# Moving the four fp16 sums of each second-layer pair from VectorE to GpSimd in an attention and mixture-of-experts kernel

## Chip, cores, metric

One NeuronCore of one Trainium2 chip. The metric is the device time of one execution in microseconds (us); lower is better. In the profile PE is TensorE's matmuls, PEld its weight loads, DVE is VectorE, ACT is ScalarE, POOL is GpSimd, SP is SyncE. The granted clock is the share of its full clock that the profile shows TensorE was given. In this kernel matmuls write tiles in PSUM (their names end in `ps`); the other tiles named below lie in SBUF.

## The reference, cut to what matters

Linear attention makes x (4608 tokens by 512), then eight experts of two layers follow, each weighted by a gate P that a balancing loop has normalised:

```python
for e in range(E):                      # E = 8, D = 512, F = 1024
    h = np.maximum(x @ w1[e], 0.0)
    ye = h @ w2[e]
    out += P[:, e:e + 1] * ye
```

The argument is about experts 2 to 7 (counted from 0), which the kernel runs from about 330 us on.

## The kernel before

From expert 1 on, both layers use the seven-product form of a 2x2 block product (Strassen's, in Winograd's arrangement): seven products instead of eight, paid for with sums of operands. Each expert is 6 *units*. A unit is 4 *groups* of the first layer (seven products each) and 3 *pairs* of the second layer (a pair is two blocks of 128 tokens, seven products each). The pairs of one unit run interleaved with the groups of the next unit.

A pair needs four sums of first-layer outputs, all SBUF to SBUF in fp16:

```python
class Pair:
    ...
    def sums(self, earlier=None):
        ...                                     # S1, S2, S4: two buffers each
        for out_, in0, in1, op in (
            (S1[:], self.a21, self.a22, ALU.add),
            (self.a21, self.a11, self.a21, ALU.subtract),     # in place in H
            (S2[:], S1[:], self.a11, ALU.subtract),
            (S4[:], self.a12, S2[:], ALU.subtract),
        ):
            i = (nc.gpsimd if self.last else ve).tensor_tensor(
                out=out_, in0=in0, in1=in1, op=op
            )
            ...
```

So before the change only the very last pair has its sums on GpSimd. The products P7 (reads the in-place `a21`), P6 (S2), P5 (S1) and P3 (S4) follow in a fixed order on TensorE.

VectorE has other SBUF-to-SBUF sums: three for the second-layer weights of each expert (called *V sums* here; 128x1024, made at the expert's first pair), one difference in w2, and 16 for the first-layer weights (*w1 sums*, written to tiles T or in place to w1e; 128x256; 12 of them in the last unit of the expert before):

```python
        if name == "P1":
            if self.first:                      # first pair of an expert
                tw2[0:2] = [t_pool.tile(... name=f"V{k_}")[:] for k_ in (2, 3)]
                ve.tensor_tensor(out=tw2[0], in0=b22, in1=b12, op=ALU.subtract)
                ve.tensor_tensor(out=tw2[1], in0=tw2[0], in1=b11, op=ALU.subtract)
            self.mult(self.U, self.a11, b11, True)
            se.copy(out=self.W, in_=self.U)
            if not self.last:
                self.sums()
        elif name == "P7":
            if self.first:
                tw2[2:3] = [t_pool.tile(... name="V4")[:]]
                ve.tensor_tensor(out=tw2[2], in0=b21, in1=tw2[0], op=ALU.subtract)
            self.mult(self.V, self.a21, tw2[1], self.last)
        ...
```

A group ends its products in one PSUM bank Z (shown as `p_ps`), which VectorE empties twice with a fused add and relu before TensorE may go on there:

```python
        product(Z, T3, x_part(1, 0, n), True)
        add_relu(h22, Z, u4)          # VectorE: H <- relu(p_ps + u), line 744
        ...
        product(Z, T4, x_part(1, 1, n), False)   # in the next group
        add_relu(h21, Z, u2)
```

VectorE also adds each product, gated, to the result (`acc <- rows_ps, P_tok, acc`, line 814). From expert 1 on the order on each engine is chosen by the scheduler when the program is built; only dependencies bind it.

## Time and profile before

| | before |
|---|---|
| median of 2 runs | 987.89 us (987.68 to 988.11) |
| PE busy, 330 to 970 us | 639.87 of 640 us |
| DVE busy, same stretch | 545.12 us (85%) |
| POOL busy, same stretch | 7.42 us |

The page of the kernel before: engines' busy time over the span, and the first line of the chain that ended last.

```profile
PE 968.0 (98%) x7846; PEld 677.9 (69%) x7846; DVE 810.4 (82%) x1838; ACT 566.4 (57%) x1260; POOL 60.4 (6%) x82
...
PE 93%; DMA 2%; DVE 2%; ACT 1%; POOL 1%; issue 0%; DVEq 0%; POOLq 0%; ACTq 0%; SPq 0%
```

Windows of the kernel before: stretch, its length, busy time of PE, PEld, DVE, ACT, POOL (and instructions), granted TensorE clock, DMA share, GB/s. The first lies in mid-expert, the second holds the start of an expert's second layer.

```profile
434.00:440.00 6.00, 6.00 (x48) 4.52 (x47) 3.96 (x9) 3.04 (x8) 0.00 (x0) 1.00 0.35 101
440.00:446.00 6.00, 6.00 (x47) 4.35 (x46) 6.00 (x14) 3.49 (x9) 0.23 (x1) 1.00 0.00 0
```

TensorE has no gap in either, even where VectorE is busy for 6.00 of 6 us.

The sums that stay on VectorE, kernel before: nanoseconds minimum/median/maximum.

```profile
L846 DVE TENSOR_TENSOR V<-w2e x7: 680/681/684, 219.0 to 879.9; 128x1024 f16<-128x1024 f16 x7
L847 DVE TENSOR_TENSOR V<-V,w2e x7: 683/685/687, 220.0 to 880.9; 128x1024 f16<-128x1024 f16 x7
L856 DVE TENSOR_TENSOR V<-w2e,V x7: 680/684/687, 223.1 to 884.4; 128x1024 f16<-128x1024 f16 x7
...
L722 DVE TENSOR_TENSOR T<-w1e,T x24: 284/288/299, 301.1 to 862.0; 128x256 f16<-128x256 f16 x24
```

Timeline of the kernel before around the V sums of expert 3, VectorE: start, length, engine, line, operation, out<-in.

```profile
439.36 0.55 DVE L744 CUSTOM_DVE_ANT_0 H<-p_ps,u 128x384 f16<-128x384 f32 x1
439.83 0.47 DVE L814 SCALAR_TENSOR_TENSOR acc_lo<-rows_ps,P_tok,acc_lo 128x256 f32<-128x256 f32 x1
440.22 0.68 DVE L846 TENSOR_TENSOR V<-w2e 128x1024 f16<-128x1024 f16 x1
440.82 0.42 DVE L829 TENSOR_TENSOR hs<-H 128x512 f16<-128x512 f16 x1
441.15 0.69 DVE L847 TENSOR_TENSOR V<-V,w2e 128x1024 f16<-128x1024 f16 x1
441.75 0.42 DVE L829 TENSOR_TENSOR H<-H 128x512 f16<-128x512 f16 x1
442.09 0.42 DVE L829 TENSOR_TENSOR hs<-hs,H 128x512 f16<-128x512 f16 x1
442.42 0.55 DVE L744 CUSTOM_DVE_ANT_0 H<-p_ps,u 128x384 f16<-128x384 f32 x1
```

The same place on TensorE:

```profile
443.03 0.48 PE L109 MATMUL p_ps<-xT,T 128*128 128x384 f16 x2
```

VectorE runs two V sums, three pair sums (L829) and then the relu (L744), which is over at 442.97; the matmul into `p_ps` that waits for it starts at 443.03, on time. There is no slack left, but nothing is late.

### The profile page before, as it was taken

The page shows a single profiled execution, that of the slowest core. Times are in us where ns is not written, and L with a number is a line of the kernel's source. Part 1 is how long each engine was busy: PE and PEld are TensorE (multiplying, and loading weights), DVE is VectorE, ACT ScalarE, POOL GpSimd, SP SyncE. Part 2 cuts the span into 40 slices and gives each one's busy share as a digit, 9 for nine tenths or more (in the row PEclk, how much of TensorE's full clock was granted, in tenths as well). Part 3 has the DMA queues.
Part 4 walks back from the last instruction along what each step waited for, and adds up shares of the span by engine and source line. Part 5 has one row for each costly group of instructions (what it writes and reads, how often), then busy time and mean ns, then how long its engine had stood idle before and what let it go on. Part 6 is the DMA issues. An engine that isn't in the chain of part 4 may idle for free.

```text
span 987.4 us, 20228 instructions
## 1 busy us (share of the span) xinstructions
PE 968.0 (98%) x7846; PEld 677.9 (69%) x7846; DVE 810.4 (82%) x1838; ACT 566.4 (57%) x1260; POOL 60.4 (6%) x82
## 2 busy tenths in 40 slices
PE   7999999989999999999999999999999999999997
PEld 6445544447777777777777777777777777777775
DVE  5886774779889888988789888988789888988887
ACT  5756665467776555555555555555555555555551
POOL 6302110010000000000000000000000000000001
PEclk8999999999999999999999999999999999999999
DMA  9969981642013410133113400233103400104535
GB/s 168 206 99 154 160 153 26 125 67 67 26 48 68 75 42 25 38 79 67 42 33 68 88 29 25 51 66 68 49 25 68 92 25 27 48 25 114 131 86 128
DMA packets 80336, 73.54 MB, mean 74 GB/s; under 512 B 33264, under 2 KB 72176, under 8 KB 80240
## 3 DMA queue, kind: packets, MB, share of 16 engines
q0 software_dynamic: 27232, 30.94, 19.9%
q1 hardware_dynamic: 52768, 41.06, 16.9%
q8 instruction: 61, 1.00, 0.4%
q14 instruction: 35, 0.29, 0.1%
q10 hardware_dynamic: 240, 0.26, 0.1%
HBM read 83.12 MB, written 12.98 MB: 97 GB/s over the span
## 4 chain that ended last, share of the span: by engine, by line
PE 93%; DMA 2%; DVE 2%; ACT 1%; POOL 1%; issue 0%; DVEq 0%; POOLq 0%; ACTq 0%; SPq 0%
PE rows_ps L109 34%; PE h_ps L109 28%; PE copied_ps L109 11%; PE p_ps L109 11%; PE y_ps L109 5%; PE small_ps L109 4%; DMA v_ld<-in_v_dram 2%; DMA q_pT<-q_p 1%; DVE xT L109 0%; DVE acc_hi L814 0%; POOL hs_last L829 0%; DVE P_tok L109 0%; DMA out_dram<-acc_lo 0%; DVE colp L109 0%; ACT u L109 0%
## 5 line engine op out<-in xcount | busy, mean ns | idle before, releaser
L814 DVE SCALAR_TENSOR_TENSOR acc_lo<-rows_ps,P_tok,acc_lo 128x512 f32<-128x512 f32 (+1 forms) x322 | 203.7, 642 | 74.5 <-PE rows_ps L109 74.4
L109 PEld LDWEIGHTS <-H 128*128 128x128 f16 x2080 | 203.0, 98 | 83.1 <-issue 1.2
L750 ACT CAST u<-h_ps 128x384 f16<-128x384 f32 x288 | 137.8, 478 | 131.2 <-PE h_ps L109 130.6
L109 PEld LDWEIGHTS <-w1e 128*128 128x128 f16 x1632 | 156.3, 98 | 67.9 <-issue 7.8
L744 DVE CUSTOM_DVE_ANT_0 H<-p_ps,u 128x384 f16<-128x384 f32 x329 | 181.7, 552 | 6.6 <-PE p_ps L109 6.4
L109 PEld LDWEIGHTS <-hs 128*128 128x128 f16 x1500 | 146.6, 98 | 56.2
L109 PE MATMUL h_ps<-S,w1e 128*128 128x384 f16 x672 | 164.1, 326 | 1.1 <-ACT u L109 0.9
L109 PE MATMUL p_ps<-xT,T 128*128 128x384 f16 x672 | 164.1, 326 | 0.1
L109 PE MATMUL h_ps<-xT,w1e 128*128 128x384 f16 (+1 forms) x616 | 150.3, 351 | 1.4 <-DVE xT L109 1.3
L109 PE MATMUL rows_ps<-V,H 128*128 128x256 f16 x1000 | 150.0, 273 | 0.7 <-DVE acc_hi L814 0.7
L109 PE MATMUL rows_ps<-w2e,hs 128*128 128x256 f16 x1000 | 150.0, 273 | 0.0
L782 ACT ACTIVATE H<-h_ps 128x384 f16<-128x384 f32 x144 | 70.7, 491 | 95.0 <-PE h_ps L109 95.0
L109 PEld LDWEIGHTS <-T 128*128 128x128 f16 x1008 | 98.1, 98 | 29.2 <-issue 2.8
L109 PE MATMUL rows_ps<-w2e,H 128*128 128x256 f16 (+1 forms) x568 | 91.2, 285 | 0.0
L763 ACT COPY copied_ps<-h_ps 128x384 f32<-128x384 f32 x144 | 67.5, 468 | 35.2 <-PE h_ps L109 35.2
L773 ACT ACTIVATE H<-copied_ps 128x384 f16<-128x384 f32 x144 | 70.9, 492 | 20.3 <-PE copied_ps L109 20.3
L109 PE MATMUL h_ps<-S,T 128*128 128x384 f16 x336 | 81.8, 325 | 0.3 <-ACT copied_ps L109 0.3
L109 PE MATMUL copied_ps<-xT,w1e 128*128 128x384 f16 x336 | 82.1, 326 | 0.0
L109 PE MATMUL copied_ps<-w2e,H 128*128 128x256 f16 x504 | 75.5, 272 | 0.0
L109 PE MATMUL rows_ps<-V,hs 128*128 128x256 f16 x500 | 75.0, 272 | 0.0
L814 DVE SCALAR_TENSOR_TENSOR acc_lo<-copied_ps,P_tok,acc_lo 128x256 f32<-128x256 f32 x126 | 60.3, 479 | 0.4
L814 DVE SCALAR_TENSOR_TENSOR acc_hi<-rows_ps,P_tok,acc_hi 128x512 f32<-128x512 f32 (+1 forms) x56 | 41.3, 738 | 20.1 <-PE rows_ps L109 19.3
(135 smaller groups left out, 957.5 us busy)
## 6 DMA issues: line engine op xcount, KB each, us to landing
S<-x_saved SPq DMA_DIRECT2D x108, 192.0 KB, 2.4
out_dram<-acc_lo SPq DMA_DIRECT2D x62, 128.0 KB, 2.4
w1e<-in_moe_w_dram POOLq DMA_DIRECT2D x7, 1024.0 KB, 9.3
w2e<-in_moe_w_dram POOLq DMA_DIRECT2D x7, 1024.0 KB, 10.0
k_ld<-in_k_dram POOLq DMA_DIRECT2D x16, 288.0 KB, 8.4
v_ld<-in_v_dram POOLq DMA_DIRECT2D x16, 288.0 KB, 9.4
q_ld<-in_q_dram POOLq DMA_DIRECT2D x16, 288.0 KB, 7.8
x_saved<-S SPq DMA_DIRECT2D x18, 192.0 KB, 1.9
```

The source lines that it names most:

```text
L109: i = getattr(self.engine, name)(*args, **kwargs)
L744: latest = ve._custom_dve(TENSOR_ADD_SAT, out=out, in0=ps[:, 0:TU], in1=t[:], s0=FP32_MAX, s1=0.0)
L750: se.copy(out=t[:], in_=ps[:, 0:TU])
L763: se.copy(out=Y[:, 0:TU], in_=X[:, 0:TU])
L773: se.activation(out=h11, in_=Y[:, 0:TU], func=AF.Relu)
L782: se.activation(out=h12, in_=X[:, 0:TU], func=AF.Relu)
L814: ve.scalar_tensor_tensor(out=a, in0=rows, scalar=P_tok[:, g, self.e : self.e + 1], in1=a, op0=ALU.mult, op1=ALU.add,)
```

## The change

The intent is to relieve VectorE, the second busiest engine, by giving the four sums to GpSimd, which is nearly idle, from the third expert on (e = 2).

```diff
@@ -826,7 +826,7 @@
                 (S2[:], S1[:], self.a11, ALU.subtract),
                 (S4[:], self.a12, S2[:], ALU.subtract),
             ):
-                i = (nc.gpsimd if self.last else ve).tensor_tensor(
+                i = (ve if self.e == 1 else nc.gpsimd).tensor_tensor(
                     out=out_, in0=in0, in1=in1, op=op
                 )
                 if self.last and earlier is not None:
```

It moves 107 pairs, 428 instructions. In the built program the order of TensorE, ScalarE and SyncE is unchanged. On VectorE the scheduler now puts the three V sums in a row, all three ahead of the relu, and in the last unit of an expert it shifts some w1 sums, the w2 difference and a relu against each other. So the change has two parts, another engine and another order.

## The prediction

> **What bounds the kernel now.** TensorE. The busy-time windows give PE 99.97 of every 100 us between 300 and 900 us (DVE 85 to 87, ACT 56, POOL under 2); the chain of waits is 93% PE. A unit of three pairs and four groups takes 17.92 us in the timeline, 5.97 us a pair, with no PE gap. So the moved work is not on the critical path: VectorE waits for TensorE (83 us for rows_ps after 300 us, in the waits), never the other way round. There is nothing to gain beyond a fraction of a microsecond in the tail.
>
> **What moves.** 107 pairs (experts 2 to 7, the last pair being on GpSimd already) times four 128x512 fp16 sums: 0.42 us each on DVE, 1.15 us each for the four on POOL at the end of the trace. DVE loses about 180 us of busy time, POOL gains about 493 us: 4.7 of each 5.97 us. TensorE, ScalarE and DMA orders are unchanged; the two weight loads per expert stay in POOL's queue with tens of us to spare.
>
> **Latency.** Mid-unit pairs may start their sums 5 us early, so 4.7 us is hidden. A unit's first pair waits for the last relu of its H (513.1 us in the timeline): on POOL S2 ends about 3.5 us later, at 516.7; the matmul that needs it loads weights at 517.1. It just fits: 0 to 0.2 us lost.
>
> **Tail.** The last three pairs come 3.5 us apart there, but POOL needs 4.7 us for each. The last pair's sums start near 979.5 instead of 977.0: +2.5 us.
>
> **Port.** The Trainium skill ("SBUF — State Buffer", Who interferes with whom) says a DVE instruction with two SBUF inputs contends with a GpSimd instruction that reads SBUF, and that the second "fully blocks". The trace of before has no such overlap, so no run here shows it; during the last pair's POOL sums DVE ran accumulations with one PSUM input at normal length, which agrees with the rest of the rule. What is left on DVE with two SBUF inputs: per expert three V sums (0.68 us, now back to back in DVE's order, right where the first pair's sums run), one w2 difference (0.68), 16 w1 sums (0.29), these in the last unit and the start of the next, where DVE was already 17.8 of 18 us busy. If they take turns with 1.15 us POOL sums, each waits up to 1.15 us. Estimate: the three V's end about 3 us late (445.5 instead of 442.3), the relu behind them holds p_ps, and TensorE stalls about 3 us; six experts, 18 us. The 12 sums of the last unit stall it another 2 to 5 us, for five experts: 10 to 25 us. The accumulations and relus between have slack of 0.05 to 1 us only.
>
> **Time.** 987.9 + 2.5 (tail) + about 30 (port, stage boundaries) = 1020 us. Without the lock, 989 to 992. Range 991 to 1045. Chances: faster by over 2% 0.01, same 0.33, slower 0.66.
>
> **What would show it.** Right: DVE groups of V, w2e, T (w1) sums with means well above 0.68 and 0.29 us, up to 1.8 and 1.4; the STT and relu groups unchanged; PE idle on the relu into H (p_ps) in the units around each expert change, PE still 99.9% busy in the middle units; POOL about 50% busy; tail 2 to 3 us longer. Wrong: V and T sums at their old durations.
>
> **What would make it wrong.** No blocking, or DVE gets the port in the middle of a POOL sum: then only the tail remains. POOL sums longer than 1.15 us beside a busy DVE: a unit's first pair then has no slack, and every unit stalls. A GpSimd that keeps the port over consecutive sums: then stalls double.

## The result, and the profile after

| | before | after |
|---|---|---|
| median of 2 runs | 987.89 us (987.68 to 988.11) | 1028.38 us (1027.81 to 1028.94) |
| ratio | | 1.041, 95% interval 1.0365 to 1.0455 |
| granted TensorE clock, profiled run | 0.996 | 0.985 |

A ratio is the mean time of one kernel's fast runs over the mean time of the other's fast runs of the same rounds, so it is not quite the ratio of the medians. The change makes the kernel 40 us slower; a repeat on another chip gave 1027.37 us beside 989.63 us, ratio 1.0386.

The page after, the same two lines:

```profile
PE 984.6 (96%) x7846; PEld 683.3 (67%) x7846; DVE 718.7 (70%) x1410; ACT 567.5 (55%) x1260; POOL 556.5 (54%) x510
...
PE 76%; DVE 9%; POOL 7%; issue 4%; DMA 3%; ACT 1%; POOLq 0%; DVEq 0%; ACTq 0%
```

The same 7846 matmuls now show 984.6 us busy instead of 968.0, and the chain runs through VectorE and GpSimd for a sixth of the span. That chain does not yet say whose fault it is: it names GpSimd both where its sums are late and where VectorE stood waiting behind them.

Windows after; the start of expert 3's second layer now lies at 447 us.

```profile
440.00:446.00 6.00, 6.00 (x48) 4.47 (x47) 3.85 (x7) 3.09 (x8) 3.08 (x3) 1.00 0.24 68
446.00:452.00 6.00, 4.67 (x36) 3.37 (x35) 5.71 (x6) 2.97 (x7) 4.30 (x4) 1.00 0.12 34
452.00:458.00 6.00, 5.12 (x27) 3.36 (x27) 3.70 (x8) 1.45 (x3) 5.64 (x5) 0.72 0.00 0
458.00:464.00 6.00, 6.00 (x48) 4.51 (x47) 3.64 (x7) 3.50 (x8) 5.09 (x6) 1.00 0.73 100
```

In mid-expert TensorE is as gapless as before, with GpSimd making all the sums. At the start of the second layer it first stands still and then, in the next window, runs 27 matmuls instead of 48 at a mean granted clock of 0.72.

The sums that stayed on VectorE, after (answers to the four lines of before):

```profile
L846 DVE TENSOR_TENSOR V<-w2e x7: 681/1473/1537, 220.3 to 912.5; 128x1024 f16<-128x1024 f16 x7
L847 DVE TENSOR_TENSOR V<-V,w2e x7: 682/1523/1525, 221.2 to 914.0; 128x1024 f16<-128x1024 f16 x7
L856 DVE TENSOR_TENSOR V<-w2e,V x7: 681/1632/1634, 224.3 to 915.5; 128x1024 f16<-128x1024 f16 x7
...
L722 DVE TENSOR_TENSOR T<-w1e,T x24: 279/842/1076, 302.3 to 894.2; 128x256 f16<-128x256 f16 x24
```

Timeline after, VectorE, GpSimd and TensorE one after the other; the brackets give the idle time before an instruction and what ended it.

```profile
446.92 0.55 DVE L744 CUSTOM_DVE_ANT_0 H<-p_ps,u 128x384 f16<-128x384 f32 x1
447.38 0.47 DVE L814 SCALAR_TENSOR_TENSOR acc_lo<-rows_ps,P_tok,acc_lo 128x256 f32<-128x256 f32 x1
447.78 1.47 DVE L846 TENSOR_TENSOR V<-w2e 128x1024 f16<-128x1024 f16 x1
449.28 1.52 DVE L847 TENSOR_TENSOR V<-V,w2e 128x1024 f16<-128x1024 f16 x1
450.73 1.63 DVE L856 TENSOR_TENSOR V<-w2e,V 128x1024 f16<-128x1024 f16 x1
452.28 0.54 DVE L744 CUSTOM_DVE_ANT_0 H<-p_ps,u 128x384 f16<-128x384 f32 x1
```

```profile
447.55 1.15 POOL L829 TENSOR_TENSOR hs<-H 128x512 f16<-128x512 f16 x1 [4.39 <-DVE H L744]
448.78 1.48 POOL L829 TENSOR_TENSOR H<-H 128x512 f16<-128x512 f16 x1
450.22 1.59 POOL L829 TENSOR_TENSOR hs<-hs,H 128x512 f16<-128x512 f16 x1
451.89 1.48 POOL L829 TENSOR_TENSOR hs<-H,hs 128x512 f16<-128x512 f16 x1
```

```profile
450.19 0.49 PE L109 MATMUL h_ps<-xT,w1e 128*128 128x384 f16 x2
452.88 0.48 PE L109 MATMUL p_ps<-xT,T 128*128 128x384 f16 x2 [2.21 <-DVE H L744]
453.20 0.77 PE L109 MATMUL rows_ps<-V,H 128*128 128x256 f16 x4
453.76 0.85 PE L109 MATMUL h_ps<-S,T 128*128 128x384 f16 x2
```

Read the first two together. The V sum that starts at 447.78 inside a GpSimd sum is not done until 449.25, 0.55 us after that sum's end at 448.70. The GpSimd sum begun at 448.78 lasts 1.48 us instead of 1.15 and ends 1.01 us after the V sum. They take turns through all three V sums. VectorE works in order, so the relu behind them comes at 452.28, and the matmul that needs the emptied bank waits 2.2 us. The matmuls after it are longer (2 of 384 columns in 0.85 us instead of 0.48).

**Where the 40 us lie.** Both programs issue the same matmuls in the same order, so the k-th matmul of one trace can be set beside the k-th of the other. Between the 2000th matmul and the last, the delay grows by 38.1 us, in steps at three kinds of place:

| place | steps | each | sum |
|---|---|---|---|
| V sums, start of each second layer, experts 2 to 7 | 6 | 2.3 us waiting, then 1.6 us of half-speed matmuls | 23.3 us |
| last unit of experts 2 to 6, where the w1 sums are made | 5 | 2.3 us waiting (0.4 + 1.2 + 0.4 + 0.3) | 11.5 us |
| tail, last three pairs | 1 | 2.7 us | 2.7 us |

The sum is 37.5 us; the rest is in steps below 0.3 us and at the start and end of the span. The half speed is in the clock record: six stretches of 3.413 us at 0.5 of full clock, one behind each V place (3.413 x 0.5 = 1.7 us lost; 1.6 us shows in the matmuls). The trace of before has none from 30 us on but for the last instants.

The tail after, TensorE: the bracket names GpSimd, and here it is a late result, not a turn.

```profile
1013.90 0.61 PE L109 MATMUL rows_ps<-V,H 128*128 128x256 f16 x4 [0.66 <-POOL H L829]
1015.01 0.61 PE L109 MATMUL rows_ps<-V,hs 128*128 128x256 f16 x4 [0.50 <-POOL hs L829]
...
1018.71 0.61 PE L109 MATMUL p_ps<-V,H 128*128 128x256 f16 x4 [0.78 <-POOL H L829]
```

### The profile page after: what moved, and what is told of

Read it like the earlier page. It is cut to its first block, busy times and chain, and to the rows that moved or that the text cites. A ratio compares the mean times of both kernels' runs of the same rounds, so it can differ in the third digit from the quotient of the medians.

```text
span 1027.2 us, 20469 instructions
## 1 busy us (share of the span) xinstructions
PE 984.6 (96%) x7846; PEld 683.3 (67%) x7846; DVE 718.7 (70%) x1410; ACT 567.5 (55%) x1260; POOL 556.5 (54%) x510
## 4 chain that ended last, share of the span: by engine, by line
PE 76%; DVE 9%; POOL 7%; issue 4%; DMA 3%; ACT 1%; POOLq 0%; DVEq 0%; ACTq 0%
PE rows_ps L109 27%; PE h_ps L109 23%; PE copied_ps L109 9%; PE p_ps L109 9%; POOL hs L829 5%; PE y_ps L109 5%; PE small_ps L109 4%; DVE acc_lo L814 2%; POOL H L829 2%; DVE T L722 2%; DMA v_ld<-in_v_dram 2%; DVE H L744 1%; DMA k_ld<-in_k_dram 1%; DVE V L856 1%; DVE w1e L722 1%
## 5 line engine op out<-in xcount | busy, mean ns | idle before, releaser
L814 DVE SCALAR_TENSOR_TENSOR acc_lo<-rows_ps,P_tok,acc_lo 128x512 f32<-128x512 f32 (+1 forms) x322 | 206.4, 642 | 130.3 <-PE rows_ps L109 129.9
L829 POOL TENSOR_TENSOR hs<-H 128x512 f16<-128x512 f16 x107 | 123.8, 1157 | 164.8 <-DVE H L744 160.6
L109 PEld LDWEIGHTS <-hs 128*128 128x128 f16 x1500 | 148.7, 99 | 61.3 <-issue 3.9
L109 PE MATMUL p_ps<-xT,T 128*128 128x384 f16 x672 | 164.5, 326 | 21.2 <-DVE H L744 21.2
L829 POOL TENSOR_TENSOR hs<-H,hs 128x512 f16<-128x512 f16 x107 | 127.8, 1194 | 11.9 <-PE rows_ps L109 5.2
L829 POOL TENSOR_TENSOR H<-H 128x512 f16<-128x512 f16 x108 | 126.6, 1173 | 8.2
L829 POOL TENSOR_TENSOR hs<-hs,H 128x512 f16<-128x512 f16 x107 | 126.4, 1181 | 0.0
L127 POOL DMA_DIRECT2D w1e<-in_moe_w_dram x11 | 8.5, 773 | 167.4 <-PE h_ps L109 128.9
L109 PE MATMUL h_ps<-S,T 128*128 128x384 f16 x336 | 84.0, 332 | 0.4 <-ACT copied_ps L109 0.3
```

Of the source, the lines that this page charges most:

```text
L109: i = getattr(self.engine, name)(*args, **kwargs)
L127: nc.gpsimd.dma_start(out=w[0][:, :, f0:f1], in_=view[:, :, f0:f1])
L814: ve.scalar_tensor_tensor(out=a, in0=rows, scalar=P_tok[:, g, self.e : self.e + 1], in1=a, op0=ALU.mult, op1=ALU.add,)
L829: i = (ve if self.e == 1 else nc.gpsimd).tensor_tensor(out=out_, in0=in0, in1=in1, op=op)
```

## The experiments

Three theories were to be told apart:

- **Port**: VectorE instructions with two SBUF inputs and GpSimd's sums take turns; VectorE is thrown back, its relu is late, TensorE waits and, after a long wait, gets half clock.
- **Latency**: GpSimd's sums are 2.8 times as long as VectorE's (1.15 us against 0.42), so TensorE waits for their results.
- **Order**: the scheduler now puts three V sums in a row ahead of the relu; that alone makes it late, whatever GpSimd does.

Each kernel differs from the changed kernel or the kernel before in one point; quiet and quiet2 put several together. The diffs are set against the changed kernel or the kernel before, whichever is nearer. "Matmul lag" is the growth of the delay against the trace of before, measured as above, in us.

| run | median, beside before in the same rounds | ratio (95%) | V places | w1 places | tail | lag |
|---|---|---|---|---|---|---|
| changed kernel | 1028.38, 987.89 | 1.041 | 6 x 2.3, 6 half clocks | 5 x 2.3 | 2.7 | 38.1 |
| first_dve | 1007.09, 990.33 | 1.0173 (1.0158 to 1.0188) | 6 x 0.47 | 5 x 2.3 | 2.7 | 17.0 |
| first_only | 1007.84, 990.33 | 1.0184 (1.0165 to 1.0202) | 6 x 2.3, 2 half clocks | 0 | 0 | 17.2 |
| v4_late | 1008.23, 990.33 | 1.0181 (1.0166 to 1.0197) | 6 x 0.75 | 5 x 2.3 | 2.7 | 18.7 |
| no_v (wrong result) | 1004.55, 990.33 | 1.0142 (1.0127 to 1.0158) | 0 | 5 x 2.3 | 2.7 | 13.8 |
| write_only (wrong result) | 999.74, 989.68 | 1.0098 (1.0083 to 1.0113) | no stall of the relu | none of the relu | see text | 9.9 |
| read_one (wrong result) | 1053.27, 989.68 | 1.0635 (1.0617 to 1.0653) | see text | see text | 4.9 | 62.7 |
| unit_dve | 1009.72, 989.68 | 1.0198 (1.0183 to 1.0213) | 6 x 2.3, 2 half clocks | 0 | 2.7 | 20.2 |
| quiet | 992.74, 989.68 | 1.0027 (1.0012 to 1.0042) | 6 x 0.47 | 0 | 0 | 3.1 |
| quiet2 | 991.70, 989.63 | 1.0017 (1.0005 to 1.003) | 0 | 0 | 0 | 0.3 |
| tail_only | 993.12, 989.63 | 1.0036 (1.0023 to 1.005) | 0 | 0 | 2.8 | 2.8 |
| after_again (changed kernel) | 1027.37, 989.63 | 1.0386 (1.0372 to 1.04) | 6 x 2.3, 5 half clocks | 5 x 2.3 | 2.7 | 36.0 |

### first_dve: the first pairs back on VectorE

```diff
-                i = (ve if self.e == 1 else nc.gpsimd).tensor_tensor(
+                i = (ve if self.e == 1 or self.first else nc.gpsimd).tensor_tensor(
```

> As the changed kernel, but the sums of the first pair of each of experts 2 to 7 (6 pairs of 107) stay on VectorE, where they stood before. Theory (port): the three V sums no longer meet a GpSimd sum, so they are back at 0.68 us and the stall of 2.3 us and the 1.56 us of half clock behind it are gone at all six experts: 6 x 3.9 = 23 us less, about 1005 us; the 2.3 us at each of five w1 places and 2.7 us in the tail stay. Rival (latency: what TensorE waits for is GpSimd's slower sums themselves, everywhere a pair starts): 6 of 107 pairs changed, so at most a few us less, about 1025 us.

1007.09 us. Six pairs of 107 bring back 21 us of the 38 (lag 38.1 to 17.0). Latency is out as the main cause. The 2 us missing to 1005 have a reason of the same kind: the third V sum now meets the *second* pair's sums (1.23 us instead of 0.68) and 0.47 us is lost at each expert.

### first_only: only the first pairs on GpSimd

```diff
-                i = (nc.gpsimd if self.last else ve).tensor_tensor(
+                i = (nc.gpsimd if self.last or self.first and self.e > 1 else ve).tensor_tensor(
```

> As the kernel before, but the sums of those 6 first pairs (and of the last, as before) are on GpSimd, 101 pairs stay on VectorE. Port theory: V sums at about 1.5 us, six stalls of 3.9 us: 988 + 23 = 1011 us, no loss at the w1 places, no loss in the tail. Latency rival: 6 of 107 of the loss, about 990 us. If 1011 and first_dve at 1005 both hold, the cost sits wholly at these 6 pairs and adds.

1007.84 us; 17 us instead of the 23 expected. The six waits of 2.3 us are all there, with V sums of 1.47, 1.52 and 1.63 us as in the changed kernel, but half clock followed only two of them. So the waits belong to these six pairs, and the half clock is a matter of chance or phase; see after_again.

### v4_late: the order changed, GpSimd untouched

```diff
                 if self.first:
                     tw2[2:3] = [t_pool.tile([P, FH, DH], F16, name="V4")[:]]
-                    ve.tensor_tensor(out=tw2[2], in0=b21, in1=tw2[0], op=ALU.subtract)
+                    i = ve.tensor_tensor(out=tw2[2], in0=b21, in1=tw2[0], op=ALU.subtract)
+                    if self.e > 1:
+                        not_before(latest, i)
```

> As the changed kernel, all sums on GpSimd, but from the third expert on the third V sum is held behind the relu that stood behind it (order only, one edge). Port theory: two V sums still take turns with GpSimd, the relu comes 1.6 us earlier, so TensorE waits about 0.7 us instead of 2.3 us at each expert and the gap is too short to bring the half clock: 6 x 3.1 = 18 us less, about 1010 us; half-clock stretches gone from the trace. Latency rival: GpSimd's sums are untouched, so no change, 1028 us. If the half clock comes for another reason than the long gap, it stays and the time is about 1019 us.

1008.23 us: one ordering edge for one of three V sums is worth about 20 us (lag 38.1 to 18.7) with every pair sum still on GpSimd. The wait is 0.74 us at five experts and 0.81 at one, and no half clock follows. V sums two at a time are still 1.47 and 1.52 us. This refutes latency a second time, and shows that the harm is done through the relu behind the V sums.

### no_v: the V sums left out

```diff
-                if self.first:
+                if self.first and self.e == 1:      # at both places of V sums
```

> Wrong result on purpose: as the changed kernel, but the V sums of experts 2 to 7 are not made (those of expert 1 are used again), all pair sums on GpSimd. Port theory: nothing of VectorE with two SBUF inputs meets the first pair's sums; TensorE does not wait there: about 1005 us, with the w1 places (11.5 us) and the tail (2.7 us) left. Latency rival: the first pair's sums come as late as ever, so 1028 us less at most 1 or 2 us. This one does not tell the port from plain VectorE load; the runs with a GpSimd that only writes do.

1004.55 us, result wrong (relative error 1.95). No step is left at the V places; the w1 places and the tail are as they were. All first pairs still had their sums on GpSimd, so these do come in time.

### write_only: GpSimd writes but does not read

```diff
-                i = (ve if self.e == 1 else nc.gpsimd).tensor_tensor(
-                    out=out_, in0=in0, in1=in1, op=op
-                )
+                if self.e == 1 or self.last:
+                    i = (ve if self.e == 1 else nc.gpsimd).tensor_tensor(
+                        out=out_, in0=in0, in1=in1, op=op
+                    )
+                else:
+                    for _ in range(2):
+                        i = nc.gpsimd.memset(out_, 0.0)
+                        after(latest, i)
```

> Wrong result on purpose: each of the four GpSimd sums of a pair is replaced by two memsets of its output tile (GpSimd writes SBUF and reads none), started by the same kind of relu; VectorE's order (three V sums in a row ahead of the relu) is that of the changed kernel. Port theory, as the skill words it (a DVE instruction with two SBUF inputs contends only with a GpSimd instruction that reads): V sums back at 0.68 us and w1 sums at 0.29 us, no stalls at the experts, 988 to 993 us. Rival (order: the three V sums in a row ahead of the relu are the cause, whatever GpSimd does): about 1010 us or more. Rival (any GpSimd work takes the port): V sums still lengthened, time between 1000 and 1028 us.

999.74 us, result wrong (0.98). The time missed the expected range, but the question was answered. The V sums of write_only, in the same row ahead of the relu as in the changed kernel (line numbers are shifted by 5):

```profile
L851 DVE TENSOR_TENSOR V<-w2e x7: 679/681/682, 219.8 to 888.5; 128x1024 f16<-128x1024 f16 x7
L852 DVE TENSOR_TENSOR V<-V,w2e x7: 684/692/693, 220.7 to 889.3; 128x1024 f16<-128x1024 f16 x7
L861 DVE TENSOR_TENSOR V<-w2e,V x7: 682/685/685, 223.8 to 889.9; 128x1024 f16<-128x1024 f16 x7
```

All eighteen of experts 2 to 7 began while a memset was running, and none took more than 0.693 us; no w1 sum took more than 0.294 us. VectorE's instructions other than the pair sums stand in exactly the order of the changed kernel, at the w1 places too. That takes away "order" and "any GpSimd work" at both kinds of place. (The rule named in the expectation is the one that the prediction takes from the skill.) The 10 us come from elsewhere: the memsets were tied to a later relu than the sums are and take 8 x 0.52 us a pair, so weight loads waited for `hs` in 37 places; the waits for the relu are gone. TensorE's weight loads, write_only:

```profile
PEld L109 <- POOL hs L835: 19.5, 37, 1.1
```

### read_one: GpSimd reads one input instead of two

```diff
-                i = (ve if self.e == 1 else nc.gpsimd).tensor_tensor(
-                    out=out_, in0=in0, in1=in1, op=op
-                )
+                ...                                   # e == 1 and the last pair as before
+                    i = nc.gpsimd.tensor_scalar(
+                        out=out_, in0=in0, scalar1=0.5, scalar2=None, op0=ALU.mult
+                    )
```

> Wrong result on purpose: each GpSimd sum is replaced by a GpSimd product with a constant, one SBUF input instead of two, same VectorE order. Port theory: it still reads SBUF, so V sums are still lengthened, by about the length of one such instruction each (perhaps 0.5 to 1.1 us); stalls in between, 995 to 1025 us. If reading with one input does not contend, as write_only.

1053.27 us, result wrong (0.90): slower than the change itself, and far outside what I expected. I had taken a one-input instruction to be shorter. It is longer; groups of GpSimd, read_one (count, busy us, mean ns), then what TensorE's matmuls waited for after 325 us (total us, times, longest):

```profile
L834 POOL TENSOR_SCALAR hs<-H 128x512 f16<-128x512 f16 x214 | 318.9, 1500 | 80.2 <-PE rows_ps L109 55.6 <-DVE acc_hi L814 18.9 <-DVE H L744 5.5
```

```profile
PE rows_ps L109 <- POOL H L834: 29.8, 36, 2.4
PE rows_ps L109 <- POOL hs L834: 19.0, 36, 0.8
```

Four of 1.49 us are 6.0 us, about the whole 6.1 us of a pair; 35 of the 36 units lose 1.55 to 1.94 us each, and the last, the tail, 4.9. This is what the latency theory looks like when it is true: waits for `H` and `hs` of GpSimd, in every unit. In the changed kernel, at 1.15 us each, waits for GpSimd's sums are 2.8 us in 5 places, all in the tail (1.0 for `hs` and 1.0 for `H` into rows_ps, 0.8 into p_ps), against 21.2 us for the relu (here its three longest lines):

```profile
PE p_ps L109 <- DVE H L744: 21.2, 21, 2.3
PE rows_ps L109 <- DVE acc_lo L814: 1.0, 4, 0.3
PE rows_ps L109 <- POOL hs L829: 1.0, 2, 0.5
```

read_one also shows how long the turn is. VectorE sums that began while the one-input instruction was less than 0.47 us old were held until it was about that old (w2 difference begun 0.26 us into it: 0.89 us instead of 0.68; w1 sum begun 0.21 us into it: 0.54 instead of 0.29), and those that began later (0.48 to 1.4 us into it) ran at their normal length. The exception is the third V sum of each expert: it began 0.49 to 0.52 us into a GpSimd instruction that had itself been held up by the second V sum (1.9 us instead of 1.49), and took 1.10 us instead of 0.68. So an instruction that had not been held up kept VectorE out for about a third of its 1.49 us.

### unit_dve: the pairs beside the w1 sums back on VectorE

```diff
-                i = (ve if self.e == 1 else nc.gpsimd).tensor_tensor(
+                on_ve = self.e == 1 or self.n == NU - 2 and self.e < E - 1
+                i = (ve if on_ve else nc.gpsimd).tensor_tensor(
```

> As the changed kernel, but the sums of the three pairs of the fifth unit of experts 2 to 6, those that run while the next expert's w1 sums are made, stay on VectorE (15 pairs). Port theory: the w1 and w2 sums are back at 0.29 and 0.68 us there and the 2.3 us lost at each of five places are gone: 11.5 us less, about 1017 us; six V stalls and the tail stay. Rival (VectorE load: VectorE has too much to do there): VectorE gets 5 us more work there, so no gain or a loss.

1009.72 us; the lag is 18 us less than the change's although only 11.5 were expected. The five w1 places are free of waits, as expected, while VectorE does *more* there. The other 6 us: only two of the six V waits were followed by half clock, against six (4 x 1.6 us).

### quiet and quiet2: GpSimd only where VectorE has no such sums

```diff
+                on_ve = (
+                    self.e == 1 or self.first                      # quiet2: self.n == 0 and self.i < 2
+                    or self.n == NU - 2 and self.e < E - 1
+                    or self.n == NU - 1 and self.e == E - 1 and not self.last
+                )
-                i = (ve if self.e == 1 else nc.gpsimd).tensor_tensor(
+                i = (ve if on_ve else nc.gpsimd).tensor_tensor(
```

> Both of these together, and the two pairs before the last on VectorE as before: 84 pairs stay on GpSimd, only where VectorE does no sums of two SBUF inputs. Port theory: everything lost comes back, 987 to 989 us, equal to the kernel before and no faster, since TensorE was without gaps there. Latency rival: still most of the 40 us lost.

> As quiet, with the second pair of each of experts 2 to 7 on VectorE too (78 pairs stay on GpSimd): in quiet the third V sum met that pair's sums (1.23 us instead of 0.68) and TensorE lost 0.47 us at each expert. Port theory: V sums all at 0.68 us, no TensorE gap over 0.3 us between 330 us and the tail, ratio to the kernel before 0.999 to 1.001. If another cost of having sums on GpSimd exists, the ratio stays near quiet's 1.003.

quiet: 992.74 us, ratio 1.0027, so not quite equal: 6 x 0.47 us for the third V sum meeting the second pair's sums. quiet2 takes those away too, and the lag against before is 0.3 us; the list of what TensorE's matmuls waited for is empty between 330 and 970 us, as it is for the kernel before. Windows of quiet2 and of before over that stretch:

```profile
330.00:970.00 640.00, 639.79 (x4892) 477.19 (x4891) 451.05 (x909) 357.56 (x805) 363.18 (x321) 1.00 0.25 58
```

```profile
330.00:970.00 640.00, 639.87 (x4893) 478.04 (x4891) 545.12 (x1222) 356.77 (x804) 7.42 (x9) 1.00 0.26 57
```

94 us less work on VectorE, and TensorE's 640 us do not move. This shows both halves for this stretch: GpSimd's sums cost TensorE no time here, where they meet almost no VectorE sum (five w1 sums still do, 1.07 us instead of 0.29, and nobody waits for them), and relieving VectorE brings nothing. No version was faster than the kernel before, and none could be by this route, since TensorE has no gap to give up.

The expected ratio of quiet2 was 0.999 to 1.001; 1.0017 (1.0005 to 1.003) was measured. Its trace is 2.2 us longer than that of before; 0.3 us of this lies behind the 2000th matmul (near 215 us) and 2.0 us ahead of it, where both programs have the same instructions in the same order on every engine. In some profiles, quiet2's among them, one more half-clock stretch lies near 55 us and costs about 1.2 us; in the profile of before it is absent. So in the profiled run the excess is not a cost of the moved sums. One of the five timed runs, with a granted clock of 0.997, took 989.52 us, inside the range of before (988.43 to 990.17); the other four, at 0.995, took 991.25 to 992.13 and were 1 to 2 us above the three runs of before at 0.995. Why these four were longer is not settled.

### tail_only

```diff
-                i = (nc.gpsimd if self.last else ve).tensor_tensor(
+                on_pool = self.n == NU - 1 and self.e == E - 1
+                i = (nc.gpsimd if on_pool else ve).tensor_tensor(
```

> As the kernel before, but the two pairs before the last one (last unit of the last expert) have their sums on GpSimd: only the tail is changed. Port theory plus latency in the tail: 2.7 us longer, ratio 1.0027; TensorE there waits for GpSimd's sums (pairs 3.5 us apart, four sums 4.7 us). If the tail cost came from the port, none of it: ratio 1.000.

Ratio 1.0036, lag 2.8 us, with TensorE waiting for `H` and `hs` of GpSimd (0.41, 0.50, 0.65, 0.50 and 0.77 us). In the tail it is latency: with no first-layer groups in between, pairs come 3.5 us apart and four sums take 4.7 us.

### after_again: the half clock

> The changed kernel once more, on the chip of these runs, for the half clock: the other kernels' 2.4 us gaps brought it only where one gap lay wholly (69% or more) in one window of the clock record's 3.413 us grid, 2 of 6 times in two kernels, against 6 of 6 in the changed kernel, whose experts are 116.05 us apart, 34.0 windows. If that is a lock-in of the phase, it comes again: 4 to 6 stretches, 1025 to 1029 us, and every gap with an idle share of 0.69 or more is followed by one, none with 0.61 or less. If it was chance: 1 to 3 stretches, about 1020 to 1023 us.

1027.37 us, five half-clock stretches in six. In each of the four traces below these stretches begin on a grid of 3.413 us and last one step of it. For each TensorE gap of about 2.4 us (from 0.16 us after the start of the last matmul to the start of the next) I took the share of one grid step that it fills:

| trace | idle share of the fuller step, experts 2 to 7 | half clock follows |
|---|---|---|
| changed kernel | 0.72, 0.69, 0.69, 0.69, 0.70, 0.70 | all six |
| after_again | 0.72, 0.68, 0.66, 0.64, 0.64, 0.63 | the first five |
| first_only | 0.71, 0.37, 0.45, 0.57, 0.69, 0.37 | first and fifth |
| unit_dve | 0.61, 0.70, 0.35, 0.47, 0.59, 0.70 | second and sixth |

The line lies near 0.63 or 0.64 (about 2.2 of 3.41 us) in these traces. The gaps of 0.8 to 1.2 us at the w1 places and in v4_late fill at most 0.35 of a step and never bring it. In the changed kernel these gaps are 116.2 us apart, 34.0 steps, so a gap that once lies well in a step does so at the next expert again. In first_only and unit_dve they are 112.2 us apart (32.9 steps) after a gap without half clock and 113.9 us (33.4 steps) after one with it, and the gap wanders over the edge.

The rule holds more widely if all of TensorE's idle time in a grid step is added up, and not that of one gap alone (a matmul of 384 columns counted as 0.16 us, its spacing in the traces, others in proportion). In all thirteen traces together, 31 full-clock steps were idle for 0.645 of their length or more, and half clock followed every one; 3711 were idle for 0.64 or less, and it followed none. The 31 have other causes too: read_one's 2.4 us wait for a GpSimd sum in the tail, and the step near 51 us that precedes the stretch near 55 us (idle for 0.70 in quiet2, 0.67 in the changed kernel, 0.55 in before).

So the 2.3 us at the w1 places also set the phase at which the V gaps fall; that would be why unit_dve gained more than its own 11.5 us. This last step is inferred from these distances; no run shifted the phase alone.

## Why the prediction was right

The forecast was 1020 us (991 to 1045), slower by over 2% with 0.66; 1028.38 us came. Point by point:

- **TensorE bounds the kernel, nothing to gain.** Right, and shown by quiet2.
- **Hidden latency of mid-unit pairs; a unit's first pair just fits.** Right: middle units stay at 6.00 busy of 6.00 us. read_one shows how narrow it was: 1.49 us instead of 1.15 and every unit loses 1.55 us.
- **Tail +2.5 us.** 2.7 us, and 2.8 us alone in tail_only.
- **Port.** The prediction rested on the Trainium skill, "SBUF — State Buffer", section "Who interferes with whom": a VectorE instruction with two SBUF inputs contends with a GpSimd instruction that reads SBUF, not with one that only writes it. That the loser "fully blocks", which the prediction quotes too, that section says of another case; for two SBUF inputs it stands in the page's "Summary: rules for kernel authors". The trace agrees on both sides: 1.47 to 1.63 us instead of 0.68 beside sums, 0.68 to 0.69 beside memsets; accumulations (0.48 and 0.75 us) and relus (0.55 us), whose other input is in PSUM, are unchanged.
- **V places: "TensorE stalls about 3 us; six experts, 18 us".** The term was mis-sized: the wait is 2.3 us (13.9 us in all). The three V sums are lengthened by 0.79, 0.84 and 0.95 us, 2.6 us together, and the relu has about 0.3 us to spare in the new order (in write_only it ends at 444.98 us and the matmul starts at 445.24). What it left out is the half clock, 6 x 1.6 us = 9.5 us; together 23.3 us.
- **w1 places: "another 2 to 5 us, for five experts: 10 to 25 us".** 2.3 us each, 11.5 us.
- **Sum: "about 30 (port, stage boundaries)".** 35 us. The missed half clock (9.5 us) and the overestimated V wait (4 us) partly cancel, which is luck. Of the 8 us by which the point came out low, 5 are here; most of the rest is 1.2 us in the profiled run ahead of the 2000th matmul, where nothing was changed, and steps below 0.3 us.
- **Mis-sized without effect.** "A unit ... takes 17.92 us" is wrong: the w2 differences of successive experts are on average 109.96 us apart in the trace of before, 18.33 us a unit. And VectorE did not lose 180 us: its busy time fell by 92 us. The records of instructions that run back to back overlap, so that about 48 us of the moved 180 had not counted before, and 41 us of waiting for the port now count as busy. POOL gained 496 us, as predicted (493).

## What to carry to other kernels

Before work goes to GpSimd, list the VectorE instructions that will run beside it and have two SBUF inputs: in the changed kernel each of them that began during a GpSimd sum waited for its turn, and what is harmed is whatever stands behind them in VectorE's order, here a relu that TensorE needed. Look first at whether the engine that is relieved is on the critical path at all. A late wait of 2 us on TensorE can cost nearly twice its length through the clock, so breaking one wait into two short ones, or moving one instruction behind the urgent one (one edge: 20 us here), may be worth more than removing work.

## What the Trainium skill lacked or had wrong

- "SBUF — State Buffer", section "SBUF: two separate sides", says that whoever starts first gets the shared pair for the whole instruction, for two SBUF inputs too. Here, by the starts that the profile shows, a GpSimd product with a constant (one input, 128x512 fp16, 1.49 us) held off VectorE's two-input sums only during its first 0.47 us or so; a two-input sum (1.15 us) did so for 1.0 to 1.06 us.
- "GPSIMD Engine Reference", Engine selection, calls one-input instructions "roughly line-rate". Here the one-input product takes 1.49 us on 128x512 fp16, longer than the two-input sum (1.15 us); a memset takes 0.52 us. Its factor of about 2 to VectorE is 2.8 for this fp16 sum (1.15 against 0.42 us).
- "TensorE: Matmul & The Clock Gate", section "HAM oscillation", warns of idle gaps over about 3.4 us. Here gaps of 2.4 us brought half clock for 3.413 us in every gap that left 0.64 or more of one step of the 3.413 us grid idle, and in none with 0.63 or less (24 gaps in four traces); with all idle time of a step added up the line lies between 0.640 and 0.645 (31 steps with half clock behind them, 3711 without, thirteen traces). That the window is free-running and that long, as the page's "What's actually happening" says, agrees with the record: within a trace all stretches lie on one grid.
- No page that I read says that the phase of that window can lock to the period of a kernel's loop (six of six and five of six gaps hit at 116.2 us, 34.0 windows, against two of six at 112.2 to 113.9 us); the runs here suggest it.
